# The operand loads of an attention backward pass, moved from SyncE's DMA queue to GpSimd's

## The chip, the cores and the metric

The kernel runs on one core of a Trainium2 chip. A core has five engines with an instruction stream each: TensorE (PE, matmuls), VectorE (DVE), ScalarE (ACT), GpSimd (POOL) and SyncE (SP), and 16 DMA engines that they share. A DMA is issued by one of the engines' streams; here SyncE and GpSimd issue nearly all of them. In the profile the DMAs that SyncE issues are on queue q1, those of GpSimd on queue q0. The metric is the device time of one execution in microseconds (us); less is better.

## What is computed

The reference is a transformer block with adaptive layer norm, forward and backward: the output and nine gradients, for 2048 tokens of width 512, 32 heads of width 16, and an MLP of width 1792, in bf16. The change lies in the backward pass of the attention, which is the gradient of these lines:

```python
scores = jnp.einsum('bhqd,bhkd->bhqk', q, k) * scale
p = _softmax(scores, axis=-1)
o = jnp.einsum('bhqk,bhkd->bhqd', p, v)
```

With dO the gradient of `o`, the kernel forms for each head p = exp(scale q k) again, dP = dO v, dS = p (dP - rowsum), and from these the gradients dq = dS k, dk = dS q and dv = p dO. The normalisation and the row sums are folded into the operands beforehand.

## The kernel before

The program has an opening phase, a forward phase, the attention backward pass (`attn_bwd`, line 1149) and a last phase for the projections and parameter gradients (`phase6`, line 1291). Tensors that a later phase needs lie in DRAM (`QTq_d`, `KTq_d`, `VTq_d`, `dOTq_d`, `qtm_d`, `ktm_d`, `dOp_d`).

The backward pass takes the heads in eight groups g of four, and each group in two pairs (jp = 0, 1). For a pair it runs over four column chunks c of 512 keys, and for each chunk over 16 row blocks ib of 128 queries. One (c, ib) is a unit: two scores matmuls (L1265, `st`), two exponentials on ACT (L1269, `pu`), two dP matmuls (L1218, `dp`) and one product on DVE (L1223, `ds`, 128 x 1024). Four units make a group of units (G = 4). When the fourth product is done, one DMA transpose on SyncE turns the four `ds` tiles, 128 x 4096 bf16 or 1 MB, into 32 blocks of 128 x 128 in `dsT` (L1227). The dq matmuls read `dsT` (L1199); they are taken from the list `pendq` only once more than 2 G units stand in it, so about two groups of units after their product. The matmuls for dk and dv (L1179) need no transpose. A pair has 16 groups of units, the whole pass 256 transposes.

The order on PE and SyncE is that of the program text, set by hand (`manual_schedule`); for the other engines a scheduler sets it. On every engine instructions run in order, and a wait holds up all that follow on that engine.

While a pair is computed, the operands of a later one are loaded. `pair_pieces` (L1141) makes four pieces for a pair: 32 partitions of 4 KB each (128 KB) into the masked K and V tiles m01 and m23 (`m` in the profile). `load_group` (L1121) makes seven pieces of 256 KB for a group: two each for the Q and dO tiles with features on partitions (`QTq`, `dOTq`, or slices of `q0` for even groups) and one each for K, Q and dO with tokens on partitions. In a pair with jp = 0 the list `pieces` holds the four pieces of the same group's second pair; with jp = 1 it holds the four of the next group's first pair and the seven of the next group. The last pair instead loads 12 pieces for the last phase: eight of 256 KB (`xhat1_6`, laid over m01) and four of 384 KB (`wq_6`, laid over `q0`). That makes 8 x 4 + 7 x 11 + 12 = 121 loads. Before each group of units but a pair's first one, one piece is issued (L1250 and 1251). A tile that is loaded was last read by PE in an earlier pair; the load's instruction carries a wait for that read where its engine doesn't know yet that it is over.

GpSimd has no instruction between the end of the forward phases and the load of `wmod` at L1434, which belongs to the last phase.

Of the kernel before, what the change touches and what calls it, by code (L numbers as in the profile page):

```python
# [87 lines left out]
class K:  # L88
# [1060 lines left out]
    def attn_bwd(self):  # L1149
# [7 lines left out]
        tc, nc = self.tc, self.nc  # L1157
# [3 lines left out]
        with ExitStack() as es:  # L1161
# [22 lines left out]
            def turn(g, jp, kvT):  # L1184
                h0 = 4 * g + 2 * jp
                tp = dpp.tile([P, ST, P], BF16, name="dp")
                for st in range(ST):
                    nc.tensor.transpose(tp[:, st, :], kvT[:, st * P:(st + 1) * P], self.ident[:])
                v = tp[:].rearrange("p s (t a e) -> p t s a e", t=2, a=2)
                for t, dst in enumerate((self.dk_t, self.dv_t)):  # L1190
                    d = dst[:, :, h0 * DH:(h0 + 2) * DH].rearrange("p s (a d) -> p s a d", a=2)
                    nc.scalar.copy(d, v[:, t, :, :, 0:DH])

            def dq(u, heads):
                (T, g, jp, c, ib, i, dsT) = u
                for a in heads:
                    col = (2 * jp + a) * DH
                    for sub in range(4):
                        nc.tensor.matmul(accq[:, ib, a, :], lhsT=dsT[:, (i * 2 + a) * 4 + sub, :],  # L1199
                                         rhs=T["K"][:, 4 * c + sub, col:col + DH],  # L1200
                                         start=(c == 0 and ib == 0 and a == 0 and sub == 0), stop=False,
                                         skip_group_check=True)
                if c == SC - 1 and ib == ST - 1 and 1 in heads:
                    h0 = 4 * g + 2 * jp
                    d = self.dq_t[:, :, h0 * DH:(h0 + 2) * DH].rearrange("p s (a d) -> p s a d", a=2)
                    nc.vector.tensor_scalar(d, accq[:], self.scale, None, ALU.mult)

            def kv_two():
                for u in pend[:2]:
                    kv(u)  # L1210
                (T, g, jp, c, ib, kvT, pu, ds) = pend[1]
                del pend[:2]
                return (g, jp, kvT) if c == SC - 1 and ib == ST - 1 else None

            def dP(dp, u, a):
                (T, g, jp, c, ib, kvT, pu, dsg, i) = u
                rd = slice(64 - 64 * jp, 128 - 64 * jp)
                nc.tensor.matmul(dp[:, a, :], lhsT=T["dOT"][rd, ib * P:(ib + 1) * P],  # L1218
                                 rhs=masked["VT"][2 * jp + a][rd, 512 * c:512 * (c + 1)], start=True, stop=True)

            def dS(dp, u):
                (T, g, jp, c, ib, kvT, pu, dsg, i) = u
                nc.vector.tensor_tensor(dsg[:, i], dp[:], pu[:], ALU.mult)  # L1223
                pend.append((T, g, jp, c, ib, kvT, pu, dsg[:, i]))
                if i == G - 1:
                    dsT = dtp.tile([P, 8 * G, P], BF16, name="dsT")
                    nc.sync.dma_start_transpose(dsT[:], dsg[:].rearrange("p i a k -> p (i a k)"))  # L1227
                    for i in range(G):
                        pendq.append((T, g, jp, c, ib - G + 1 + i, i, dsT))
# [3 lines left out]
            for g in range(NQ):  # L1233
                for jp in range(2):
                    pieces = []
                    if jp == 0:
                        pieces = self.pair_pieces(g, 1)
                    elif g + 1 == NQ:
                        for st in range(0, ST, 2):
                            pieces.append((self.xhat1_6[:, st:st + 2, :], self.xhat1_d.rearrange("(st p) d -> p st d", p=P)[:, st:st + 2, :]))  # L1240
                        for kt in range(self.DT):
                            pieces.append((self.wq_6[:, kt, :], self.io["A_wqkv"][kt * P:(kt + 1) * P, :]))
                    else:
                        Tn, pieces = self.load_group(g + 1)
                        pieces = self.pair_pieces(g + 1, 0) + pieces
                    kvT = kvp.tile([P, S], BF16, name="kvT")
                    for c in range(SC):
                        c0 = 512 * c
                        for ib0 in range(0, ST, G):
                            if pieces and (c or ib0):  # L1250
                                nc.sync.dma_start(*pieces.pop(0))
                            dsg = self.dsp.tile([P, G, 2, 512], BF16, name="ds")
                            for i in range(G):
                                ib = ib0 + i
                                q = slice(ib * P, (ib + 1) * P)
                                if turnq and i == 2:
                                    turn(*turnq.pop(0))
                                pu = self.pup.tile([P, 2, 512], BF16, name="pu")

                                if last:  # L1260
                                    dp = dpp.tile([P, 2, 512], F32, name="dp")
                                for a in range(2):
                                    stt = stp.tile([P, 512], F32, name="st")
                                    rs = slice(64 * jp, 64 * jp + 64)
                                    nc.tensor.matmul(stt[:], lhsT=T["QT"][rs, q], rhs=masked["KT"][2 * jp + a][rs, c0:c0 + 512],  # L1265
                                                     start=True, stop=True)
                                    if last:
                                        dP(dp, last, a)
                                    nc.scalar.activation(pu[:, a, :], stt[:], ACT.Exp, scale=self.scale)  # L1269
                                if last:  # L1270
                                    dS(dp, last)
                                last = (T, g, jp, c, ib, kvT, pu, dsg, i)
                                if i % 2 == 1 and len(pend) >= 4:
                                    r = kv_two()
                                    if r:
                                        turnq.append(r)
                                elif i % 2 == 0 and len(pendq) > 2 * G:
                                    for _ in range(4 if len(pendq) > 3 * G else 2):
                                        dq(pendq.pop(0), [0, 1])
                T = Tn  # L1280
# [263 lines left out]
```

The softmax here doesn't subtract the row's maximum and nothing guards it: scores larger than these inputs give would overflow.

## Time and profile before

| | us |
|---|---|
| Runs of the kernel before: median of 3 (lowest, highest) | 2850.8 (2848.87, 2860.52) |
| The profiled execution, own time | 2855.5 |
| Its span, first to last instruction | 2853.7 |
| Backward pass, from the first transpose's issue to the last dq matmul | 1264.0 to 2723.7 |

The groups that make the unit, from the list of the costliest groups (line, engine, operation, output<-inputs, shapes, count, then busy us and mean ns of one, then the idle time of the engine before them and what ended it):

```profile
L1269 ACT ACTIVATE pu<-st 128x512 bf16<-128x512 f32 x2048 | 1108.3, 595 | 313.8 <-PE dp L1218 279.6
L1223 DVE TENSOR_TENSOR ds<-dp,pu 128x1024 bf16<-128x1024 f32 x1024 | 1213.1, 1220 | 198.2 <-PE dp L1218 161.9
```

and the DMA queues over the whole span (packets, MB, share of the 16 engines' time):

```profile
q1 hardware_dynamic: 1299816, 379.40, 72.5%
q0 software_dynamic: 29088, 86.21, 10.4%
```

A row of a timeline gives start, length and instruction; "SPq" is SyncE issuing a DMA, "POOL ... DMA_DIRECT2D" is GpSimd issuing one. The length there is how long the issuing engine was held, not how long the data took.

### The profile page before, as it was taken

The numbers are of one execution on the slowest core, as the hardware profiler recorded it, in microseconds if no ns is written. First come the engines' busy times: TensorE is split into PE (matmuls) and PEld (weight loads), VectorE is DVE, ScalarE is ACT, GpSimd is POOL, SyncE is SP. The second block draws the span as 40 slices with busy tenths as digits, with TensorE's granted clock in tenths as the row PEclk, the third lists the DMA queues.
The fourth block names the chain that finished last, engine by engine and source line by source line (L and its number), as shares of the span: only waits on it lengthen the run. The fifth ranks groups of instructions, "written<-read, shape, count | busy, mean of one in ns | idle before, by whom it ended". The sixth has DMA issues, their size and how long they took to land. (4 is left out here: it accounts for less than half of the span.)

```text
span 2853.7 us, 72244 instructions
## 1 busy us (share of the span) xinstructions
PE 2530.8 (89%) x29963; PEld 1218.3 (43%) x30186; DVE 1787.2 (63%) x2712; ACT 2214.1 (78%) x3376; POOL 360.7 (13%) x633
## 2 busy tenths in 40 slices
PE   5999799999999989978888898888988889889887
PEld 2555455555555545723333333333333333333343
DVE  4222423323322335648898888888988889889747
ACT  4999899999999974248787777787877778778623
POOL 2244202211311223420000000000000000000021
PEclk9999899999999999989899999999999999999999
DMA  4367733511531357989999999999999999999977
GB/s 149 88 147 161 172 70 107 123 45 40 137 83 43 100 151 175 194 192 201 211 195 203 203 196 209 199 201 210 196 208 203 199 209 198 204 204 205 214 194 187
DMA packets 1331345, 472.86 MB, mean 166 GB/s; under 512 B 1266470, under 2 KB 1293608, under 8 KB 1331016
## 3 DMA queue, kind: packets, MB, share of 16 engines
q1 hardware_dynamic: 1299816, 379.40, 72.5%
q0 software_dynamic: 29088, 86.21, 10.4%
q8 instruction: 236, 3.87, 0.5%
q10 hardware_dynamic: 2112, 2.62, 0.3%
q14 instruction: 93, 0.76, 0.1%
HBM read 83.30 MB, written 67.11 MB: 53 GB/s over the span
## 5 line engine op out<-in xcount | busy, mean ns | idle before, releaser
L1269 ACT ACTIVATE pu<-st 128x512 bf16<-128x512 f32 x2048 | 1108.3, 595 | 313.8 <-PE dp L1218 279.6
L1223 DVE TENSOR_TENSOR ds<-dp,pu 128x1024 bf16<-128x1024 f32 x1024 | 1213.1, 1220 | 198.2 <-PE dp L1218 161.9
L331 ACT ACTIVATE pu<-st 128x1024 bf16<-128x1024 f32 x1024 | 955.7, 1046 | 22.5 <-PE st L328 18.0
L328 PE MATMUL st<-QTm,KTq 128*128 128x512 bf16 x1940 | 586.5, 379 | 37.2 <-ACT pu L331 7.5
L293 PEld LDWEIGHTS <-pu 128*128 128x128 bf16 x8192 | 344.9, 96 | 245.8 <-issue 20.5
L1265 PE MATMUL st<-m,q 64*128 64x512 bf16 x1024 | 371.4, 404 | 21.4 <-ACT pu L1269 9.6
L1265 PE MATMUL st<-m,QTq 64*128 64x512 bf16 x1024 | 365.0, 396 | 16.0 <-ACT pu L1269 4.4
L1218 PE MATMUL dp<-m,q 64*128 64x512 bf16 x1024 | 373.5, 408 | 0.0
L1199 PEld LDWEIGHTS <-dsT 128*128 128x128 bf16 x8192 | 241.1, 97 | 307.1 <-DMA dsT<-ds 189.8
L1218 PE MATMUL dp<-m,dOTq 64*128 64x512 bf16 x1024 | 366.4, 401 | 0.0
L293 PE MATMUL accbank<-Vaug,pu 128*128 128x17 bf16 x8192 | 349.3, 171 | 18.3 <-DVE O L301 11.4
L328 PEld LDWEIGHTS <-KTq 128*128 128x128 bf16 x2048 | 194.9, 96 | 205.8 <-issue 140.7
L1199 PE MATMUL accq<-Kg,dsT 128*128 128x16 bf16 x4096 | 143.6, 171 | 83.1 <-DMA dsT<-ds 82.8
L1199 PE MATMUL accq<-q,dsT 128*128 128x16 bf16 x4096 | 144.5, 171 | 65.6 <-DMA dsT<-ds 65.1
L1434 POOL DMA_DIRECT2D wmod<-in_w_mod_dram x6 | 4.6, 772 | 1462.1 <-DVE kvT L1182 1455.9
L1179 PE MATMUL acckv<-ds,q 128*16 128x512 bf16 x1024 | 165.3, 405 | 0.0
L1179 PE MATMUL acckv<-pu,q 128*16 128x512 bf16 x1024 | 165.3, 405 | 0.0
L1179 PE MATMUL acckv<-ds,Qg 128*16 128x512 bf16 x1024 | 162.1, 398 | 0.7 <-DVE ds L1223 0.7
L1179 PE MATMUL acckv<-pu,dOg 128*16 128x512 bf16 x1024 | 162.1, 398 | 0.0
L1218 PEld LDWEIGHTS <-q 64*128 64x128 bf16 x1024 | 90.8, 94 | 112.0 <-issue 101.4
L1218 PEld LDWEIGHTS <-dOTq 64*128 64x128 bf16 x1024 | 89.8, 94 | 103.3 <-issue 94.1
L300 DVE RECIPROCAL rl<-accbank 128x4 f32<-128x4 f32 x128 | 23.0, 179 | 164.8 <-PE accbank L293 164.7
(309 smaller groups left out, 2345.3 us busy)
## 6 DMA issues: line engine op xcount, KB each, us to landing
KTq<-KTq_d POOLq DMA_DIRECT2D x24, 512.0 KB, 3.6
duT_d<-auT POOLq DMA_DIRECT2D x4, 1792.0 KB, 8.3
aT_d<-rT POOLq DMA_DIRECT2D x4, 1792.0 KB, 13.0
KTq_d<-KTq SPq DMA_DIRECT2D x32, 128.0 KB, 2.1
QTq_d<-ev_fm SPq DMA_DIRECT2D x32, 128.0 KB, 2.4
VTq_d<-vT POOLq DMA_DIRECT2D x4, 1024.0 KB, 6.6
O_d<-O POOLq DMA_DIRECT2D x4, 1024.0 KB, 5.4
m<-KTq_d SPq DMA_DIRECT2D x32, 128.0 KB, 3.7
```

The source lines that it names most:

```text
L293: nc.tensor.matmul(acc[:, a, sub, :], lhsT=pu[:, a, sub * P:(sub + 1) * P], rhs=Vaug[:, kb, h, :], start=(kb == 0 and a == 0 and sub == 0) ...
L300: nc.vector.reciprocal(self.rl[:, st0:st0 + 4, h], acc[:, a, :, DH])
L328: nc.tensor.matmul(stt[:, a, :], lhsT=KT[:, kb * P:(kb + 1) * P], rhs=QTm[2 * jp + a][:], start=True, stop=True)
L331: nc.scalar.activation(pu[:], stt[:], ACT.Exp, scale=self.scale)
L1179: nc.tensor.matmul(acckv[r:r + DH, :], lhsT=T[n][:, ib, col:col + DH], rhs=src[:, a, :], start=(ib == 0), stop=(ib == ST - 1))
L1199: nc.tensor.matmul(accq[:, ib, a, :], lhsT=dsT[:, (i * 2 + a) * 4 + sub, :], rhs=T["K"][:, 4 * c + sub, col:col + DH], start=(c == 0 and i ...
L1218: nc.tensor.matmul(dp[:, a, :], lhsT=T["dOT"][rd, ib * P:(ib + 1) * P], rhs=masked["VT"][2 * jp + a][rd, 512 * c:512 * (c + 1)], start=Tru ...
L1223: nc.vector.tensor_tensor(dsg[:, i], dp[:], pu[:], ALU.mult)
L1265: nc.tensor.matmul(stt[:], lhsT=T["QT"][rs, q], rhs=masked["KT"][2 * jp + a][rs, c0:c0 + 512], start=True, stop=True)
L1269: nc.scalar.activation(pu[:, a, :], stt[:], ACT.Exp, scale=self.scale)
L1434: nc.gpsimd.dma_start(wmod[:], wmod_v[:, :, j * D:(j + 1) * D])
```

## The change

One call is made on another engine. The piece is taken from the same list at the same place of the program; what it copies, and how many pieces there are, stays.

```diff
                         for ib0 in range(0, ST, G):
                             if pieces and (c or ib0):
-                                nc.sync.dma_start(*pieces.pop(0))
+                                nc.gpsimd.dma_start(*pieces.pop(0))
                             dsg = self.dsp.tile([P, G, 2, 512], BF16, name="ds")
                             for i in range(G):
```

## The prediction, made before the changed kernel ran

> **What bounds the kernel now.** I read, in this order: the page (busy shares, DMA share), a table of windows with one row for each pair of heads, SyncE's own timeline, the groups and the waits inside the backward pass. Only 1264 to 2724 us of the span matter, since the diff touches nothing else.
>
> ```profile
> PE 2530.8 (89%) x29963; PEld 1218.3 (43%) x30186; DVE 1787.2 (63%) x2712; ACT 2214.1 (78%) x3376; POOL 360.7 (13%) x633
> ...
> DMA  4367733511531357989999999999999999999977
> ...
> L1199 PE MATMUL accq<-Kg,dsT 128*128 128x16 bf16 x4096 | 143.6, 171 | 83.1 <-DMA dsT<-ds 82.8
> L1199 PE MATMUL accq<-q,dsT 128*128 128x16 bf16 x4096 | 144.5, 171 | 65.6 <-DMA dsT<-ds 65.1
> ```
>
> From slice 18 on the DMA engines show 9s while PE still waits 82.8 + 65.1 = 148 us for transposed ds tiles. So the backward pass hangs on its transposes, not on arithmetic: VectorE's work there, from the groups of that stretch, is 1208 (L1223 ds) + 48 (L1182 kvT) + 11 (L1206 dq_t) = 1267 us of 1460. The windows (columns: stretch, length, busy time of PE, PEld, DVE, ACT, POOL, clock, DMA share, GB/s) give the four first pairs:
>
> ```profile
> 1264.00:1351.50 87.50, 78.23 (x1014) 31.56 (x1013) 79.33 (x70) 70.42 (x131) 0.00 (x0) 0.97 1.15 197
> 1351.50:1445.10 93.60, 81.14 (x1033) 32.38 (x1029) 78.72 (x69) 69.27 (x129) 0.00 (x0) 0.89 1.13 206
> 1445.10:1532.70 87.60, 77.43 (x1045) 32.50 (x1044) 78.97 (x70) 70.15 (x130) 0.00 (x0) 0.98 1.15 200
> 1532.70:1627.90 95.20, 79.34 (x1043) 32.08 (x1044) 79.16 (x69) 70.39 (x131) 0.00 (x0) 0.95 1.16 203
> ```
>
> Pairs with 4 loads (jp=0) take 87.5, pairs with 11 loads (jp=1) about 94, though DVE and ACT do the same work in both. SyncE's timeline (start, length, instruction) says why:
>
> ```profile
> 1281.62 69.18 SPq L1227 DMA_TRANSPOSE dsT<-ds  x13
> 1350.85 0.57 SPq L1251 DMA_DIRECT2D m<-KTq_d  x1
> 1351.52 5.00 SPq L1227 DMA_TRANSPOSE dsT<-ds  x1
> ...
> 1374.51 0.57 SPq L1251 DMA_DIRECT2D QTq<-QTq_d  x1
> 1375.17 4.97 SPq L1227 DMA_TRANSPOSE dsT<-ds  x1
> ```
>
> Thirteen transposes in a row fill 69.18 us, 5.32 each, with no gap; a load adds its 0.57 and some 0.1 around it. SyncE is full. The view of waits books 1038 us of SyncE under "DVE ds", but if SyncE sat waiting for ds, a load would vanish in that wait and the pairs would not differ. I therefore take SyncE's row of transposes as the bound: 1264.0 to 2711.3 (first and last start of L1227) is 1447 us; 255 steps of 5.32 are 1357; the remaining 90 us come with the 121 loads (60 of 128 KB, 57 of 256 KB, 4 of 384 KB).
>
> **What the Trainium skill says.** "DMA: Bandwidth & Descriptors", section "Issuing engines are not separate DMA queues": all queues run on the same 16 engines, and another issuer saves only sequencer time, usually small. Here that time is the bound, so it is not small. Same page, "Queues, rings and completion order": engines alternate between queues packet by packet. The trace agrees in one place and not in another, both at the end of the pass (GpSimd's timeline, SyncE's timeline, and the view of DMA queues for 2726.6 to 2738.1, whose columns are packets, MB and share of the engines):
>
> ```profile
> 2711.92 0.79 POOL L1434 DMA_DIRECT2D wmod<-in_w_mod_dram  x1 [1455.94 <-DVE kvT L1182]
> 2724.43 0.91 POOL L1317 DMA_DIRECT2D O_tm<-O_d  x1 [11.73 <-PE accq L1199]
> 2725.33 0.89 POOL L1318 DMA_DIRECT2D dx1b<-dx1b_d  x1
> ```
>
> ```profile
> 2726.69 11.41 SPq L1327 DMA_TRANSPOSE dqT<-dq_t  x1
> ```
>
> ```profile
> q0 software_dynamic: 871, 3.37, 90.4%
> q1 hardware_dynamic: 816, 0.20, 9.7%
> ```
>
> In the queue view there are as many packets on GpSimd's queue q0 as on SyncE's q1, but 4 KB ones against 256-byte ones, so q1 keeps 0.20 of 3.57 MB, and a transpose whose median is 1.9 us (L1327, eight of them) holds SyncE for 11.41 beside the four 1 MB loads. In 2712 to 2716.5, with the wmod load already issued, the same view shows only q1. So a q0 load gets in between two transposes, and then nearly shuts them out until q0 is empty. Page "SBUF — State Buffer", section "Who interferes with whom", warns that VectorE in a two-port mode blocks GpSimd, which writes the descriptors. No such block shows: ds reads one PSUM and one SBUF operand at 1220 ns for 1024 elements. Page "TensorE: Matmul & The Clock Gate", "What's actually happening": the clock halves after about 3.4 us idle. The windows agree: PE busy 0.00 in 2716.3 to 2720, clock 0.50 in 2720 to 2724.
>
> **The change part by part.**
> (1) Removed from SyncE: 121 issues. Excess per pair over 16 x 5.32 = 85.1: jp=0 (87.6 - 85.1) = 2.5 for 4 loads; jp=1 mean 93.5 (the seven run from 92.5 to 95.2), so 8.4 for 11; the last pair 95.6, so 10.5 for 12. Sum 8 x 2.5 + 7 x 8.4 + 10.5 = 89 us, the 90 above. This is the most that can be gained.
> (2) Added to GpSimd: 121 issues of some 0.55 us (KTq loads, L280: 539 to 702 ns), 67 us on an engine with 0.00 busy in all four rows. Nothing is queued behind them but wmod (L1434), which waits for the end of the pass anyway. Cost nothing.
> (3) The pacing goes. On SyncE a load waits its turn behind a transpose, one for each group of units. GpSimd has no transpose in its row; it waits only until PE has finished with the old content, which is at the end of the previous pair for m, and earlier for Q, K and dO. That this wait is short already is seen on SyncE: L1251's waits there come to some 8 us in all (PE dp 4.6, PE acckv 2.8). So all of a pair's loads go out at its start, 0.55 us apart: 4 x 128 KB = 0.52 MB (jp=0), 0.52 + 7 x 256 KB = 2.36 MB (jp=1), 8 x 256 + 4 x 384 KB = 3.67 MB (last pair). No consumer of the loads is late: they are used a pair later.
> (4) What the transposes lose to such a burst. Rate of q0 from the view above: 3.37 MB in 11.5 us, 293 GB/s, so 1.8, 8.1 and 12.5 us. Off go 6% leaked to q1, 0.5 us for the pause that lies between two transposes anyway, and 0.6 us that SyncE runs ahead (estimates; the DMA records show q1 idle some 0.5 us at such a boundary, and transposes at 290 GB/s after a stall against 218 before). Left: 0.8, 6.5 and 10.6 us. Bounds: 167 GB/s (q0's 0.50 MB in 2717 to 2720) with nothing off, 3.1, 14.1, 22.0; and below, nothing, if loads find room in the pauses.
> (5) A long burst idles PE. The wait is the same as before, that of L1199 for dsT, and behind it in PE's order stand the next st, dP and kv matmuls, so ACT and DVE stop too. dq of four units is taken two groups of four (some 10.7 us) after their ds, and a transpose now lands 7.7 us (median) after its issue begins, so a delay of 6.5 outruns the slack of some 3 and PE stops for about 4 us. One half-clock window of 3.4 us then costs up to 1.7 us of PE work, most of it under the transposes still queued; I take 0.6 for each of 8 long bursts, 5 us; bounds 0 and 14.
> Sum: 8 x (2.5 - 0.8) + 7 x (8.4 - 6.5) + (10.5 - 10.6) - 5 = 13.6 + 13.3 - 0.1 - 5 = 22 us gained.
>
> The profiled execution took 2855.5 (span 2853.7), the median run 2850.8, 4.7 less. 2855.5 - 22 = 2833.5; on the runs' scale about **2829**.
>
> **The rivals.**
> A, loads in bursts, a small gain (above): 2829; own range 2812 to 2845. For it: the SyncE row is full and q0 shuts out q1.
> B, loads hidden: they slip into the pauses and every step takes 5.32. All 89 us go: 2762. For it: free DMA time in the pauses, 290 GB/s reached against some 200 used. Against: the 11.41 us transpose.
> C, no change: the DMA engines, at a share of 1.13 to 1.16 in all rows, are the bound, and bytes cost the same on either queue: 2851, own range 2840 to 2862. Against: GB/s is higher (206) in the pairs with more loads.
> D, slower: the one mechanism is the burst's length. At 230 GB/s with nothing taken off and 1.7 us of clock loss for each long one: jp=0 2.3 - 2.5, jp=1 10.3 + 1.7 - 8.4 = 3.6, last 16.0 + 1.7 - 10.5 = 7.2; 8 x -0.2 + 25 + 7 = +31 us, 2881; at 167 GB/s some +70. It decides from where a 2.36 MB burst costs more than the 8.4 us that its loads cost now. For it: the slow wmod burst. Against: these loads are contiguous runs of 2 and 4 KB.
>
> **How the numbers follow.** A 0.42, B 0.14, C 0.16, D 0.28. Half a per cent is 14 us, about what a measurement tells from no change. Faster by more: B, and three quarters of A: 0.45. Within: the rest of A, most of C, a bit of D: 0.27. Slower: D but for that bit and a rest of C: 0.28. Range 2775 to 2882: it leaves out the better half of B and the worse third of D. A's own range is 2812 to 2845.
>
> **What would show it.** Step 1: no L1251 on SyncE, its transposes in unbroken rows of 5.32 outside the bursts. Step 3: L1251 on GpSimd in clumps of 4 and 11 at the pairs' starts, not one for each group. Step 4: one or two transposes of 8 to 14 us at the start of each jp=1 pair, jp=0 pairs near 86, jp=1 near 92. Step 5: the clock at 0.50 once after each long burst. Wrong if GpSimd's loads come out evenly (then B), if jp=1 pairs exceed 94 (D), or if steps of 5.3 persist with SyncE idle between them (C).

## The result and the profile after

| | us |
|---|---|
| Runs of the kernel before: median of 4 (lowest, highest) | 2851.8 (2848.87, 2860.52) |
| Runs of the changed kernel: median of 4 (lowest, highest) | 2891.97 (2891.41, 2904.71) |
| Ratio, with its 95% interval | 1.0146 [1.0111, 1.0182] |
| Span of the profiled execution, before and after | 2853.7 and 2889.6 |

The change makes the kernel some 40 us slower; the prediction was 22 us faster, and 2891.97 lies above its range of 2775 to 2882. The page of the changed kernel, with the lines that answer to those of before (engine, queues, costliest groups):

```profile
PE 2531.1 (88%) x29963; PEld 1225.8 (42%) x30186; DVE 1784.5 (62%) x2712; ACT 2215.0 (77%) x3376; POOL 425.0 (15%) x754
...
q1 hardware_dynamic: 1287128, 355.01, 69.9%
q0 software_dynamic: 36848, 110.60, 14.0%
...
L1199 PE MATMUL accq<-q,dsT 128*128 128x16 bf16 x4096 | 144.3, 171 | 95.4 <-DMA dsT<-ds 94.8
L1199 PE MATMUL accq<-Kg,dsT 128*128 128x16 bf16 x4096 | 143.6, 170 | 91.0 <-DMA dsT<-ds 90.8
```

The work is the same (PE 2531.1 against 2530.8) and 24.4 MB went from q1 to q0. But PE now waits 94.8 + 90.8 = 186 us for transposed tiles, where it waited 148. GpSimd's timeline (start, length, instruction, idle time before it and what ended it) shows when the loads go out:

```profile
1533.26 1.01 POOL L1251 DMA_DIRECT2D m<-KTq_d  x2 [68.27 <-PE dp L1218]
1534.61 0.97 POOL L1251 DMA_DIRECT2D m<-VTq_d  x2 [0.33 <-PE st L1265]
1623.08 0.97 POOL L1251 DMA_DIRECT2D m<-KTq_d  x2 [87.50 <-PE dp L1218]
1624.42 0.97 POOL L1251 DMA_DIRECT2D m<-VTq_d  x2 [0.37 <-PE st L1265]
1625.38 1.09 POOL L1251 DMA_DIRECT2D QTq<-QTq_d  x2
1626.46 1.06 POOL L1251 DMA_DIRECT2D dOTq<-dOTq_d  x2
1630.32 0.54 POOL L1251 DMA_DIRECT2D Qg<-qtm_d  x1 [2.79 <-DMA m<-KTq_d]
1632.43 0.54 POOL L1251 DMA_DIRECT2D dOg<-dOp_d  x1 [1.58 <-DMA m<-KTq_d]
```

There are two kinds of clump, each released by PE's last use of the old tiles: four small loads at the boundary inside a group of heads (1533), and small and large loads together at the boundary between two groups (1623). The long clump isn't wholly one burst: its last load, `Kg`, goes out 17 us later (1649.91), when PE's L1199 has read the old tile, and for a group whose operands lie in `q0` two loads go out 12 to 13 us earlier. GpSimd also runs ahead: it issued the first 11 loads at 1137 to 1193, before the pass began. The queue view for 1627 to 1641 (packets, MB, share), inside the second clump:

```profile
DMA packets 3423, 2.79 MB, mean 199 GB/s; under 512 B 2916, under 2 KB 2916, under 8 KB 3422
...
q0 software_dynamic: 661, 2.07, 65.7%
q1 hardware_dynamic: 2761, 0.70, 44.2%
```

In 14 us the loads moved 2.07 MB, 148 GB/s, and the transposes 0.70 MB, where without a burst they move 1 MB in 5.32 us. One transpose beside it is the longest of the ten in 1600 to 1660 (ns min/median/max; then the time to landing):

```profile
L1227 SPq DMA_TRANSPOSE dsT<-ds x10: 4788/5342/15602, 1599.8 to 1658.8; - x10
...
DMA to landing us min/median/max: 6.8/8.4/19.1
```

And the windows at that place (columns as before) show the engines stopping and the clock falling:

```profile
1626.00:1632.00 6.00, 3.17 (x40) 1.19 (x36) 5.17 (x5) 3.74 (x8) 2.06 (x4) 1.00 1.05 213
1632.00:1638.00 6.00, 4.22 (x46) 2.35 (x48) 1.23 (x1) 1.16 (x3) 0.54 (x1) 0.72 1.12 219
1638.00:1644.00 6.00, 2.79 (x36) 1.06 (x32) 3.58 (x3) 4.14 (x8) 0.00 (x0) 1.00 1.27 174
1644.00:1650.00 6.00, 4.41 (x52) 1.62 (x52) 2.01 (x2) 2.17 (x4) 0.09 (x1) 0.53 1.03 194
```

DVE (third figure) does 1.23, 3.58 and 2.01 us of its 6. The following ledger serves for all kernels below. From SyncE's rows in each trace I took the first 14 pairs, from the start of a pair's first transpose to that of the next pair, and split them into the time that transposes held SyncE, the time that loads held it, and what is left, in which SyncE stood idle (some 0.1 us of it at each of the 224 transposes is the step from one instruction to the next):

| | first 14 pairs, us | transposes hold | loads hold | idle | mean of pairs jp=0 / jp=1 |
|---|---|---|---|---|---|
| before | 1269.7 | 1174.8 | 60.8 | 34.1 | 87.9 / 93.5 |
| changed | 1303.8 | 1253.6 | 0 | 50.2 | 89.9 / 96.3 |

So the change took 60.8 us of loads off SyncE, as meant, and got 78.8 us of longer transposes and 16.1 us of idle time for it: + 34.1 us, where the spans differ by 35.9 (the last two pairs cancel, + 7.2 and - 7.8). The time that a transpose holds SyncE has no waiting for products in it: in both traces each of the 256 starts after the last product that it reads has ended, in the median 1.6 us after it before and 0.9 us after the change.

### The profile page after: what moved, and what is told of

Read it like the earlier page. It is cut to its first block, busy times and chain, and to the rows that moved or that the text cites. A ratio compares the mean times of both kernels' runs of the same rounds, so it can differ in the third digit from the quotient of the medians.

```text
span 2889.6 us, 72369 instructions
## 1 busy us (share of the span) xinstructions
PE 2531.1 (88%) x29963; PEld 1225.8 (42%) x30186; DVE 1784.5 (62%) x2712; ACT 2215.0 (77%) x3376; POOL 425.0 (15%) x754
## 5 line engine op out<-in xcount | busy, mean ns | idle before, releaser
L1199 PEld LDWEIGHTS <-dsT 128*128 128x128 bf16 x8192 | 240.7, 96 | 337.4 <-DMA dsT<-ds 223.5
L1199 PE MATMUL accq<-q,dsT 128*128 128x16 bf16 x4096 | 144.3, 171 | 95.4 <-DMA dsT<-ds 94.8
L1199 PE MATMUL accq<-Kg,dsT 128*128 128x16 bf16 x4096 | 143.6, 170 | 91.0 <-DMA dsT<-ds 90.8
L1251 POOL DMA_DIRECT2D m<-KTq_d x30 | 15.1, 508 | 790.5 <-PE dp L1218 790.4
```

The lines of the kernel that those rows point to most:

```text
L1251: nc.gpsimd.dma_start(*pieces.pop(0))
```

## The experiments

The first four expectations name three theories. R, the release: GpSimd's loads cost because nothing paces them, and one at a time they would be nearly free. Q, the queue: loads on GpSimd's queue cost what they cost because of that queue, paced or not. N: the loads never were what made SyncE late, and nothing is to be had from moving them. All ratios are to runs of the kernel before on the same chip. In the edits, a line taken out with `nc.gpsimd` is one of the changed kernel, one with `nc.sync` one of the kernel before.

**One load at a time on GpSimd (e1_paced).** A one-element copy on GpSimd, from the last group's `ds` into the tile to be loaded, holds each load back until DVE has got there. The tiles are the same, and the load overwrites the element.

```diff
-                                nc.gpsimd.dma_start(*pieces.pop(0))
+                                d, sr = pieces.pop(0)
+                                r0 = row_of.pop(0)
...
+                                nc.gpsimd.tensor_copy(first, prev[r0:r0 + 1, 2, 0, 0:1])
+                                nc.gpsimd.dma_start(d, sr)
```

> All 121 loads stay on GpSimd, but each is held back by a one-element copy on GpSimd from the ds tile of the group of units just before it into the tile to be loaded, so that one load goes out for each group of units as in the program text. Theory R (run-ahead: the loss comes from loads that go out together): the bunches are gone, no transpose is held for more than some 7 us, and the 0.66 us that each load takes from SyncE is saved; 2770 to 2800 us. Theory Q (queue: a load on GpSimd's queue costs the transposes more than one on SyncE's, whatever its spacing): about as the changed kernel, 2880 to 2895. Theory N (SyncE was never the bound, so nothing was to be gained): 2845 to 2860.

Measured: 2825.12 us (2808.08 to 2829.67), ratio 0.9872 [0.9831, 0.9914]. Same queue, same bytes, 67 us less than the changed kernel. Q and N fall; R has the right side, but the gain (27 us) is smaller than the 50 to 80 it gave. The last pair alone got worse: 100.9 us against 95.6 before (from its first transpose's start to its last one's, and one period of 5.3 more).

**No loads (e2_no_loads, and e8_no_loads_b without its fault).** 109 of the 121 loads are left out in the first, 102 in the second, so that the pass works on the operands of other heads. In the first, the last pair's loads went into a tile that PE still read, and SyncE waited for it: that pair took 112.9 us. The second keeps the last group's loads as well.

```diff
-                        Tn, pieces = self.load_group(g + 1)
-                        pieces = self.pair_pieces(g + 1, 0) + pieces
+                        Tn, pieces = self.load_group(g + 1) if g + 2 == NQ else (self.T0, [])
...
-                                nc.sync.dma_start(*pieces.pop(0))
+                                pc = pieces.pop(0)
+                                if jp and g + 2 >= NQ:
+                                    nc.sync.dma_start(*pc)
```

> Leaves out 109 of the 121 loads (all but the last pair's 12, which stay on SyncE): every group of heads computes with the operands of the first. It prices the loads on SyncE. Theories R and Q: 255 steps of 5.32 us and 12 loads, so 109 x 0.7 = 76 to 80 us less than before, 2770 to 2780. Theory N: the pace is set elsewhere and little changes, 2835 to 2855.

> 102 of the 121 loads are left out (so the pass works on operands of other heads and its output isn't the gradient); the seven of the last group and the 12 of the last pair stay on SyncE. This repeats e2_no_loads without its fault, that the last pair's loads went into a tile still in use. If the first prediction's price of a load on SyncE is right (8 pairs of 2.5 us and 7 of 8.4, less the 6 us of the seven loads kept: 70 us), 2778 to 2788. If a good part of the loads was hidden after all: above 2800.

Measured: 2799.04 us, ratio 0.9791 [0.9762, 0.982], and 2789.6 (2782.38 to 2795.28), ratio 0.9786 [0.9764, 0.9808]. The first is above the 2770 to 2780 of R and Q by about what its fault cost (112.9 against 95.6). In the second, with 102 loads gone, the kernel is 63.6 us faster than the 2853.18 beside it. The expectation wrote 70, but its own prices give 8 x 2.5 + 7 x 8.4 - 6 = 73, so the loads were priced some 15% too high. The second to the thirteenth pair, without any load, take 85.4 us in the mean, which is 16 times 5.34. So loads on SyncE were on the path. This run doesn't tell whether by SyncE's time or by the bytes, since both went; e1_paced does, where the bytes stay. The queue view of this kernel for 60 us without a load is the yardstick for the later ones:

```profile
DMA packets 47815, 12.25 MB, mean 204 GB/s; under 512 B 47808, under 2 KB 47808, under 8 KB 47808
```

**The bursts on SyncE (e3_sp_burst).** The kernel before, with all loads of a pair issued back to back ahead of its second group of units.

```diff
-                            if pieces and (c or ib0):
+                            while pieces and (c or ib0):
                                 nc.sync.dma_start(*pieces.pop(0))
```

> All loads on SyncE as before, but a pair's 4, 11 or 12 loads are issued one behind the other ahead of the pair's second group of units. Theory R, if bunching alone is what costs: the bunch holds up the transposes for some 10 us as in the changed kernel, but on SyncE nothing is saved either, so 2880 to 2930. Theory Q (only the mixing of two queues costs): SyncE's time is the same sum as before, 2845 to 2860.

Measured: 2846.82 us (2842.0 to 2855.41, ten runs), ratio 0.9975 [0.9956, 0.9993]. The same clumps on the transposes' own queue cost nothing more than spread loads: in the ledger 1263.3 us for 14 pairs, against 1269.7. They stand at the boundary too, since on SyncE the place ahead of the second group of units lies just ahead of the pair's first transpose. So here a burst does harm on GpSimd's queue and not on SyncE's. Whether any second queue would do the same, or only this one, whose transfers the profile lists as software_dynamic, no run shows: the queue of a third engine was not tried.

**The small loads alone (e4_m_only).** Only the 60 loads of 128 KB go to GpSimd, so only the bursts of four are left.

```diff
-                                nc.gpsimd.dma_start(*pieces.pop(0))
+                                (nc.gpsimd if pieces[0][0].shape[0] == 32 else nc.sync).dma_start(*pieces.pop(0))
```

> Only the 60 loads of 128 KB (K and V tiles) go to GpSimd, the rest stays on SyncE. Theory R: 15 short bunches of four at 2.2 us each (from the changed kernel's transposes of 7.2 to 8.0 instead of 5.2) are 33 us against 60 x 0.63 = 38 saved on SyncE: 2840 to 2855; the long bunches are gone. Theory Q: 60 loads of 121 cost their share of the loss, about +20: 2865 to 2875.

Measured: 2887.61 us (2879.1 to 2894.94), ratio 1.0104 [1.0071, 1.0137]: slower than both theories said, though the long bursts, on which the prediction had put its loss, are not there. A burst of 0.52 MB costs 90.3 - 85.4 = 4.9 us in a pair with jp=0. The trace shows two parts. The ledger: 1298.5 = 1204.1 of transposes + 28.8 of loads + 65.6 idle; the idle time has nearly doubled. Its source, around the boundary after the burst at 1434, is in a row of PE's timeline, three of DVE's and two of ACT's:

```profile
1445.01 0.60 PE L1199 MATMUL accq<-q,dsT 128*128 128x16 bf16 x16 [4.54 <-DMA dsT<-ds]
```

```profile
1441.15 1.21 DVE L1223 TENSOR_TENSOR ds<-dp,pu 128x1024 bf16<-128x1024 f32 x1
1446.70 1.22 DVE L1223 TENSOR_TENSOR ds<-dp,pu 128x1024 bf16<-128x1024 f32 x1 [4.34 <-PE dp L1218]
1450.47 1.22 DVE L1223 TENSOR_TENSOR ds<-dp,pu 128x1024 bf16<-128x1024 f32 x1 [2.54 <-ACT dv_t L1192]
```

```profile
1449.40 0.58 ACT L1192 COPY dk_t<-dp 128x512 bf16<-128x512 bf16 x1 [2.13 <-PE dp L1188]
1449.88 0.59 ACT L1192 COPY dv_t<-dp 128x512 bf16<-128x512 bf16 x1
```

and in SyncE's (windows that part its rows):

```profile
1437.91 13.22 SPq L1227 DMA_TRANSPOSE dsT<-ds  x2
1454.41 5.55 SPq L1227 DMA_TRANSPOSE dsT<-ds  x1
```

PE stops 4.54 us for a late transpose, and DVE with it (4.34). Then comes `turn`, the 16 transposes on PE and the copies on ACT that a pair's end needs, in one of the two `dp` buffers, and DVE stops again (2.54 us). So the next group's products are late, and SyncE, which ended a transpose at 1437.91 + 13.22 = 1451.13, stands idle until 1454.41: 3.3 us. The other boundaries of this trace look the same: at 13 of the first 14 DVE stops twice, 1.9 to 6.2 us and then 1.6 to 2.5 (at one only the second time), and at all 14 SyncE stands idle after the next pair's first transpose. The second stop is booked to ACT's copy at five of them and to PE's `dp` at the others. A delay at this place is paid twice.

**The small bursts inside a pair (e5_m_mid).** The same loads on the same queue, still four at once, but held back by copies as in e1_paced until the middle (jp=0) or the last quarter (jp=1) of the pair.

```diff
+                    small = [] if jp and g + 1 == NQ else pieces[:4]
+                    pieces = pieces[len(small):]
...
+                            n = 4 * c + ib0 // G
+                            if n == (13 if jp else 8):
+                                for (d, sr), r0 in zip(small, row_of):
+                                    nc.gpsimd.tensor_copy(d[0:1, 0:1], prev[r0:r0 + 1, 2, 0, 0:1])
+                                for d, sr in small:
+                                    nc.gpsimd.dma_start(d, sr)
+                            if pieces and (n >= 5 if small else n):
+                                nc.sync.dma_start(*pieces.pop(0))
```

> Here, as in e4_m_only, only the 60 loads of 128 KB are on GpSimd, four at once, but they are released inside a pair (by the ninth group of units in a pair with jp = 0, by the fourteenth with jp = 1) and not at the boundary between two pairs. In e4_m_only a pair with jp = 0, which has nothing but this bunch, took 90.3 us (eight of them) against 85.6 with no loads: of these 4.7 us about 2.5 are transposes that hold SyncE longer (7 to 8 us in place of 5.2) and about 2.5 are SyncE standing idle for one late product right after them. Theory Q (the queue: four loads on the other queue share the engines with a transpose packet by packet, and whatever this delays is lost, wherever it happens): the pair with jp = 0 takes 89 to 91 us again, and the kernel 2880 to 2892. Theory B (the place: at the boundary the transpose that is delayed is the one that the next pair's start hangs on, so the idle time follows; inside a pair there is slack for it): the longer holding stays, the idle time goes, the pair with jp = 0 takes 87 to 88.5 us and the kernel 2845 to 2865.

Measured: 2852.56 us (2833.88 to 2856.7, twelve runs), ratio 0.9998 [0.9982, 1.0013]: 35 us less than e4_m_only, 2.3 us for each burst, with the place as the one difference but for the small copies, and inside what theory B gave. (The kernel before took 2851.97 us beside e4_m_only and 2853.18 beside this run.) The profiled execution is the fastest of the twelve by 14 us, so its pairs are shown for their parts and not for their length: 1193.5 of transposes, 27.8 of loads, 38.8 idle. Against e4_m_only the transposes hold SyncE nearly as long (1193.5 and 1204.1), and of the idle time of 65.6 little more is left than the 34.1 of before. From SyncE's rows, in the mean over the boundaries of the first 15 pairs:

| us | the transpose that meets the burst holds SyncE | SyncE idle after the next pair's first transpose |
|---|---|---|
| before (no burst; the pair's last transpose) | 5.2 | 0.2 |
| e4_m_only (the pair's last) | 7.5 | 2.5 |
| e5_m_mid (one inside the pair) | 7.0 | 0.6 |
| changed, four loads, inside a group of heads (the pair's last) | 7.6 | 2.6 |
| changed, the long clump, between two groups (the pair's last; the next holds 6.6) | 13.2 | 0.4 |

So a burst of four costs some 2 us of holding wherever it lies, and at the boundary as much again in idle time. Why the long clump is followed by little idle time was not looked into. In e5_m_mid PE and DVE still stop, as DVE's timeline after the burst at 1289 shows, but what follows runs through:

```profile
1300.12 1.22 DVE L1223 TENSOR_TENSOR ds<-dp,pu 128x1024 bf16<-128x1024 f32 x1 [4.69 <-PE dp L1218]
1302.06 13.16 DVE L1223 TENSOR_TENSOR ds<-dp,pu 128x1024 bf16<-128x1024 f32 x11 [0.72 <-PE dp L1218]
```

After 4.69 us of waiting, DVE makes 11 products in 13.16 us, 4.8 for four, while SyncE takes 5.32 for four, and so it catches up.

**All bursts inside the pair (e6_all_mid).** All 121 loads on GpSimd, the whole of a pair's loads at its ninth group of units.

```diff
-                            if pieces and (c or ib0):
-                                nc.gpsimd.dma_start(*pieces.pop(0))
+                            if 4 * c + ib0 // G == 8:
...
+                                for d, sr in pieces:
+                                    nc.gpsimd.dma_start(d, sr)
```

> All 121 loads are on GpSimd, as in the changed kernel, still all of a pair's loads at once, but released inside the pair by its ninth group of units. Theory Q (the length of the burst is lost wherever it lies): 2880 to 2900, as the changed kernel. Theory B (the place at the boundary is what costs): about 2.5 us less for each of 15 boundaries, and the longest burst no longer in front of a group's first units, so 2835 to 2860, with transposes of up to 15 us still in the trace. If pacing alone matters (theory R of the first call), it is at or above the changed kernel, since the bursts are as long.

Measured: 2903.09 us (2890.65 to 2904.42), ratio 1.0176 [1.0151, 1.0201]. The profiled execution is the fastest of the four. Here B falls, and Q, whose 2900 the result passes by 3 us, is the nearer: a long burst costs much inside a pair too. Pairs with four loads take 87.8 us, 2.4 over a pair without any, those with 11 take 98.5, 13.1 over it. 2.36 MB in 13.1 us is 180 GB/s. In the ledger the 14 pairs take 1303.9 us, as in the changed kernel (1303.8): what the short bursts gain (87.8 against 89.9) the long ones lose (98.5 against 96.3), since here all 11 loads go out together. The last two pairs make the rest: 193.6 against 182.3 us, where the 12 loads of the last pair are one burst. The first long burst, in SyncE's timeline, and the windows beside it:

```profile
1380.06 9.82 SPq L1227 DMA_TRANSPOSE dsT<-ds  x1
1389.97 15.04 SPq L1227 DMA_TRANSPOSE dsT<-ds  x1
```

```profile
1392.00:1398.00 6.00, 0.00 (x0) 0.00 (x0) 0.00 (x0) 0.00 (x0) 0.54 (x1) 0.50 0.98 189
1398.00:1404.00 6.00, 0.74 (x18) 0.64 (x20) 0.00 (x0) 0.00 (x0) 0.00 (x0) 0.50 1.18 232
```

Two transposes of 9.82 and 15.04 us in place of 5.3 each; for 12 us PE, DVE and ACT do next to nothing, and the clock is at half. The queue view for 1384 to 1400 says what the DMA engines did in that time:

```profile
DMA  7899999969999997996926921236996999989989
GB/s 29 143 211 161 178 320 202 161 44 141 113 56 63 49 56 38 79 66 35 134 41 63 177 57 45 69 90 158 208 258 211 334 337 448 338 285 280 175 278 300
DMA packets 3578, 2.57 MB, mean 161 GB/s; under 512 B 3140, under 2 KB 3140, under 8 KB 3577
```

From about 1388 to 1395 most slices move only 35 to 80 GB/s, and through the first half of that they count as nine tenths busy. The packets themselves take longer: by the same view for 1388 to 1392, 453 packets of q1 fill 91.4% of the 16 engines' 4 us, 129 ns each, where before the burst (1380 to 1381) it is 847 at 115.5% of 1 us, 22 ns each. This is the slowest of the seven long bursts. Over their 16 us they moved 161 to 209 GB/s, 186 in the mean, where the transposes alone moved 204. So the loads took their share almost wholly from the transposes.

**Where the single loads stand (e7_paced_last_sync, e12_e7_again, e9_paced_late, e10_paced_by_two, e11_even).** e7 is e1_paced with the last pair's 12 loads on SyncE; e12 is the same kernel on another chip. e9 begins with a pair's fifth group of units. e10 issues two at a time, every second group of units. e11 spreads the 15 loads of two pairs over every second group of units, and takes four of the last pair's loads a pair ahead. The edits of e7 and of e10:

```diff
                             if pieces and (c or ib0):
+                                d, sr = pieces.pop(0)
+                                if jp and g + 1 == NQ:
+                                    nc.sync.dma_start(d, sr)
+                                else:
+                                    r0 = row_of.pop(0)
+                                    nc.gpsimd.tensor_copy(d[0:1, 0:1], prev[r0:r0 + 1, 2, 0, 0:1])
+                                    nc.gpsimd.dma_start(d, sr)
```

```diff
+                            elif pieces and 4 * c + ib0 // G in (4, 6, 8, 10, 12, 14):
+                                two, pieces = pieces[:2], pieces[2:]
...
+                                for d, sr in two:
+                                    nc.gpsimd.dma_start(d, sr)
```

> e1_paced, but the last pair's 12 loads are on SyncE as in the kernel before. In e1_paced the last pair took 100.9 us against 95.6 in the kernel before. If these 12 large loads cost more on GpSimd's queue than on SyncE's: 2818 to 2822, some 5 us under e1_paced's 2825.1. If the last pair was late for another reason (it ends with the pass, so a late transpose has nothing behind it): 2824 to 2828.

> e7_paced_last_sync with each pair's first load at its fifth group of units in place of its second, one for each group from there on (so the 11 loads of a pair end with its fifteenth group). If single loads too cost more near the boundary between pairs (theory B), 2805 to 2809. If a single load costs the same everywhere, 2809 to 2814, as e7_paced_last_sync.

> e9_paced_late with two loads at a time, every second group of units from the fifth. Between the single load (15 loads of two pairs cost 5.8 us over the 170.9 of two pairs without loads, in e7_paced_last_sync) and the whole burst (15.2 us in e6_all_mid) this is the next dose. If what a transpose's period leaves over is used once per period (the engines have room for about one load beside one transpose, and what goes beyond is lost in full): pairs of 87 to 88 and 91.5 to 93.5 us, kernel 2822 to 2838. If two loads still fit: as e9_paced_late within 4 us.

> The kernel of e7_paced_last_sync once more, beside e11_even on one chip, since e9_paced_late (2823) and e7_paced_last_sync (2811) came from different chips. If the start of the loads in the pair made the 12 us between them: 2808 to 2815. If it was the chip: 2815 to 2825.

> Single loads again, but one for every second group of units over both pairs of a group of heads (eight in a pair with jp = 0, seven with jp = 1; four of the next group's operands are loaded a pair earlier), and four of the last pair's 12 loads (wq_6) go out on GpSimd one pair earlier. If the loss of a load comes from engines that have no room left beside a transpose, a transpose without a load after each one with a load lets them catch up: two pairs take 173.5 to 176 us in place of 176.7, and the kernel is 5 to 15 us under e12_e7_again. If each load costs a fixed time for itself (0.4 us, whatever stands beside it), the same within 4 us.

| | us, median (lowest to highest) | ratio to before |
|---|---|---|
| e7_paced_last_sync | 2811.07 (2804.98 to 2815.91) | 0.9861 [0.9838, 0.9884] |
| e12_e7_again | 2818.46 (2811.55 to 2826.08) | 0.9879 [0.9859, 0.9899] |
| e9_paced_late | 2823.2 (2813.52 to 2834.09) | 0.9884 [0.9855, 0.9912] |
| e10_paced_by_two | 2833.8 (2827.64 to 2836.88) | 0.992 [0.9895, 0.9946] |
| e11_even | 2826.92 (2816.49 to 2839.2) | 0.99 [0.9879, 0.992] |

e7 beats both kernels: about 35 to 42 us under the kernel before. Its ledger is 1237.1 us for 14 pairs: 1199.8 of transposes, no loads, 37.3 idle. Of the 60.8 us of loads it gives 25.0 back as longer transposes. It lies below both of its ranges; in its trace the last pair takes 94.7 us, 6.2 less than in e1_paced, and the rest of the 14 us between the two is in parts that the edit doesn't touch. Its PE waits for transposed tiles are the two lines' 125 us, and the queue view for 60 us with six loads among the transposes shows more moved per time than without any (217 GB/s against 204), where over the same 60 us of e6_all_mid, with a whole burst, it was 186:

```profile
L1199 PE MATMUL accq<-Kg,dsT 128*128 128x16 bf16 x4096 | 143.4, 170 | 66.2 <-DMA dsT<-ds 65.4
L1199 PE MATMUL accq<-q,dsT 128*128 128x16 bf16 x4096 | 144.2, 170 | 60.1 <-DMA dsT<-ds 59.6
```

```profile
DMA packets 44590, 13.01 MB, mean 217 GB/s; under 512 B 44162, under 2 KB 44162, under 8 KB 44584
```

Two at a time (2833.8) lies between single loads and bursts, as expected. No gain was seen from a later start (e9, above what both its theories gave; e12 puts most of the difference from e7 down to the chip), so the place matters for bursts and was not seen for single loads. e11 was a miss for both of its theories: a transpose without a load between two with one wasn't seen to help. Runs of one such kernel differ by up to 23 us, so the order of e7, e9 and e11 among themselves isn't settled.

## Why the prediction was wrong

**What bounds the kernel** was right. SyncE's row of transposes is the bound: the products are ready before each transpose starts, and without loads a pair takes 16 times 5.34 us (e8). What sets the 5.3 us, SyncE or the transfers that it issues, was not separated; that a burst on the other queue lengthens them speaks for the transfers.

**Step 1**, 89 us for 121 issues on SyncE, was some 15% too high: 102 loads were worth 63.6 us where the same prices give 73.

**Step 2**, GpSimd's issues at nothing, holds: 534 ns each in the trace of after, and nothing behind them but more loads.

**Step 3** was right in kind and wrong in place. The loads come in clumps, but GpSimd runs as far ahead as the tiles allow, so the long clump goes out at the boundary between two groups of heads and not at the start of the pair with jp=1, and each clump lies across the end of a pair. That place has a price, which the prediction didn't have: SyncE's idle time rose by 16.1 us over 14 pairs in the changed kernel, by 31.5 in e4_m_only, and by 4.7 when the same small bursts lay inside the pair (e5).

**Step 4 is the one that failed, and by its size.** The mechanism, that a burst on q0 shuts out the transposes, was right; the loss was put at 0.8 and 6.5 us for the two kinds of burst, with q0 at 293 GB/s and allowances for pauses, for SyncE's lead and for the rate after a stall (for the short burst they leave 0.6, not the 0.8 written). Against the 14 pairs of e8 the transposes of the changed kernel hold SyncE 92 us longer, where step 4 gave 7 x (0.8 + 6.5) = 51; this is most of the error. By the table above a short burst makes one transpose 2.4 us longer, and a long clump makes two longer by 8.0 and 1.4. The idle time, 14 us more than in e8, had no place in the sum but for the 4 us of step 5 for these pairs. Together the pairs pay 1303.8 - 14 x 85.4 = 108 us for their loads, where steps 4 and 5 gave 7 x (0.8 + 6.5 + 0.6) = 55; those 53 us are most of the 58 by which the sum was off (22 gained, 36 lost by the spans). The step's own bounds, 3.1 and 14.1 us at 167 GB/s with nothing taken off, held what a burst costs inside a pair (2.4 and 13.1 in e6), but not the short one at the boundary (4.9 in e4). The 293 GB/s came from loads at the end of the pass, with one small transpose beside them. Why the engines move so little in the mixture was not settled.

**Step 5** had the right sign and little weight: the clock falls to 0.50 to 0.72 after a long burst, but its mean over the run is 0.959, against 0.960 before. PE's stop is longer than the 4 us given, up to 10.5 us in the changed kernel by the view of waits.

**The rivals.** D, slower by the burst's length, came nearest (2881), but in part by luck. Its point of decision, the loads of a pair with jp=1 costing more than 8.4 us, was passed: 96.3 - 85.4 = 10.9. But it lacked the boundary: the small bursts, which it priced at 0.2 us less than before, cost 2 us more (89.9 against 87.9), and for the last pair it had 7.2 us more where it took 7.8 less. The small bursts are alone enough for nearly the whole loss when the large loads stay on SyncE (e4). Of B's gain less than half could be had, and only with single loads (e1, e7). C fell with e1 and e7, where the same bytes on the other queue cost less; e8 didn't decide it, since there the bytes went too.

## What to carry to other kernels

- A queue that is full with transfers in order also paces what is issued between them. Whoever moves transfers off it has to pace them again on the new engine, here with a one-element copy that depends on the producer; the same move then goes from 40 us lost to 27 gained (e1), and to 35 to 42 with the last pair's loads left where they were (e7, e12).
- Price a burst on a second queue by its bytes at the rate that the mixture has been seen to reach, with nothing taken off for spare bandwidth, and look at where it is released: here the wait for a freed buffer put it on the boundary between two pairs, where the pipeline had least slack.

## What the runs showed of the hardware that was not expected

- Bursts of 2.36 MB beside transposes on another queue moved, both queues together, 161 to 209 GB/s over 16 us each (e6), while the transposes alone moved 204 (e8) and single loads among them 217 (e7). In the slowest of them the transposes' 256-byte packets took 129 ns each for 4 us, in place of 22. Bursts of the same loads on the transposes' own queue cost nothing extra (2846.8 against 2852.0).
- A transpose of 1 MB that met such a burst held its issuing engine for 13.2 us in the mean and up to 15.6 in the changed kernel, and up to 18.8 in e6, instead of 5.3.
